# Left-over score tiles of two units in one step of four 64x64 products, and the ring loads issued in the table's order

## The chip, the cores and the metric

The kernel runs on one core of a Trainium2 chip. The metric is the device time of one execution in microseconds (us). Three runs of the kernel before gave 600.52 to 601.35 us, with a median of 600.97 us. The engines are PE (TensorE; PEld is its weight load), DVE (VectorE), ACT (ScalarE), POOL (GpSimd) and SP (SyncE), which issues every DMA here; SPq is SP's queue.

## The reference

Three layers stand one behind the other, all in float32. Attention has 4 batches of 8 heads, 576 rows and head size 64; its softmax keeps only scores within tau of the row's maximum. A soft mixture of 8 experts with 4 slots each follows, and then an MLP.

```python
scores = scale * np.matmul(q, k.transpose(0, 1, 3, 2))
thresh = np.max(scores, axis=-1, keepdims=True) - tau
scores = np.where(scores >= thresh, scores, -1e9)
attn = softmax(scores)                       # written out in the reference
x = (attn @ v), heads side by side           # 2304 x 512
d = softmax(x @ phi, axis=0); slots = d.T @ x
slot_out[e] = np.maximum(slots[e] @ w1[e], 0) @ w2[e]     # 8 experts
x = softmax(x @ phi, axis=1) @ slot_out
h = x @ w_in                                  # 2304 x 2048
return (h * sigmoid(1.702 * h)) @ w_out
```

## The kernel before

**Attention** (function `attention`) works in 16 units, each of two heads of a batch. A head has 576 query rows: four chunks of 128 and 64 left over. A unit therefore has nine score tiles of 128 x 576: tiles 0 to 7 are a chunk of one head, and tile 8 is the left-over 64 rows of both heads, one above the other. For each tile the stages are: scores on PE, row maximum with a copy to SBUF on DVE (`row_max`, RM), threshold on POOL (TH), exponential on ACT (`exps`, E), mask with row sum on DVE (`mask`, MK), transposes on PE (`trans`, T), their copies on ACT (C), then products with v on PE (`attn_v`, A; with the left-over rows of v, LV) and the division by the sums on DVE (VM).

`scores` (S0 to S3) computes two tiles at once: the two heads lie in partitions 0 to 63 and 64 to 127 of `qx` and `kx`, and their products of 64 contracted rows run as a pair, each head into a PSUM tile of its own (two banks a tile, two such tiles in all). The left-over tile (L) is made by one product of 128 contracted rows with `q_left`, a 128 x 128 matrix that holds the two heads' left-over queries on its diagonal and zeros elsewhere; `prep_rest` fills the diagonal by two ACT copies of 64 x 64. Each float32 product stands in the trace as two instructions.

**What sets the order.** The table `PLAN` gives every stage of a unit a place in tile times (columns: even unit, odd unit, last unit, first unit). The calls are sorted by it, and the instructions of PE, DVE, ACT and POOL are kept in that order by `tc.keep_in_program_order`. Loads that go through `load` are kept in that order on SP too. The loads of the expert weights into rings (`load_quarters`, line 101) are not: they stand where the scheduler puts them. The rings c, d, e, ... take SBUF that attention gives back (`swap`).

**After attention** come the experts (`experts`; `acc` on lines 1034 and 1076 is layer 1 and layer 2, with weights w_a to w_m streamed in) and the MLP (`ffn`, lines 1249 and 1275 to 1277). Decoding of w_in (`raw`, `top`, `y`, `wi`) is spread through attention.

Of the kernel before, what the change touches and what calls it, by code (L numbers as in the profile page):

```python
# [19 lines left out]
def kernel(  # L20
# [64 lines left out]
    def load_quarters(ring, n, spread=False):  # L85
# [3 lines left out]
        while i < n and quarters:  # L89
# [8 lines left out]
            if spread:  # L98
                slow.append(io)
            else:  # L100
                nc.sync.dma_start(**io)
# [42 lines left out]
    first = [True]  # L144

    def load(**io):
        ins = nc.sync.dma_start(**io)  # L147
        if first[0]:
            tc.keep_in_program_order(ins)
# [95 lines left out]
    def attention():  # L245
# [29 lines left out]
        q_left = [pl.tile([P, P], F32, name="q_left") for pl in stk]  # L275
        for t in q_left:
            ve.memset(t, 0.0)
# [49 lines left out]
        def turned(u, nm):  # L327


            if (u, nm) not in qk:  # L330
                n = C * P if nm == "q" else S + R
                qk[u, nm] = stk[u % 2].tile([P, n], F32, tag=nm, name=nm + "x")
            return qk[u, nm]

        def prep_rest(u, bank):
# [7 lines left out]
            def after():  # L343

                for h in range(2):
                    own = slice(h * R, (h + 1) * R)
                    ac.copy(out=q_left[u % 2][own, own], in_=t[own, 0, :])
# [5 lines left out]
        def prep_main(u, nm, bank):  # L353
# [7 lines left out]
            def after():  # L361
                src = t.rearrange("p c t -> p (c t)")
                if nm == "q":
                    ac.activation(
                        out=turned(u, nm), in_=src, func=AF.Copy, scale=neg if u else 1.0
# [36 lines left out]

        def weights(i):
            u, t = divmod(i, TPU)
            return p2[u, t // 2][:, t % 2 * S:(t % 2 + 1) * S]

        def scores(i):
# [13 lines left out]
            else:  # L421
                s_ps[i] = ps_s.tile([P, 2, 512], F32, tag="s", name="s_ps")
                prods = [(s_ps[i], q_left[u % 2], kx[:, R:])]
# [7 lines left out]
        def row_max(i):  # L431

            u, t = divmod(i, TPU)
            if (u, t // 2) not in p2:
                p2[u, t // 2] = pp[(u * (C + 1) + t // 2) % len(pp)].tile([P, 2 * S], F32, tag="p2", name="p2")
                mns[u, t // 2] = sm.tile([P, 2], F32, tag="mn", name="mn")
            mn2 = mns[u, t // 2]
            mn = mn2[:, t % 2:t % 2 + 1]
# [7 lines left out]
        def threshold(i):  # L446
            thr[i] = sm.tile([P, 1], F32, tag="th", name="th")
# [9 lines left out]
        def mask(i):  # L457
# [3 lines left out]
            if (u, half) not in l_sb:  # L461
                l_sb[u, half] = sm.tile([P, C + 1], F32, tag="l", name="l", bufs=2)
# [30 lines left out]
        def across(u, half):  # L493
# [8 lines left out]
            def after():  # L502
                row = l_row[u, half] = ptp.tile([P, 2 * P + R], F32, tag="l_row", name="l_row", bufs=2)
                ac.copy(out=row[:, 0:2 * P], in_=ps[:, 0:2 * P])
                for h in range(2 * half):
                    own = slice(h * D, (h + 1) * D)
                    ac.copy(out=row[own, 2 * P:], in_=ps[own, 2 * P + h * R:2 * P + (h + 1) * R])
# [11 lines left out]
        def trans(i):  # L519
# [6 lines left out]
            if i >= 140:  # L526
# [10 lines left out]
            if t == 2 * C:  # L537
# [7 lines left out]
                def after():  # L545
                    products_of(u, 1)
                    ac.copy(
                        out=pt[u, 1][:, :, :, 2 * P:].rearrange("p h c r -> p c h r"),
                        in_=ps.rearrange("p c (h r) -> p c h r", h=2),
                    )  # L550
# [841 lines left out]
```

## Time and profile before

| | us |
|---|---|
| median of 3 runs | 600.97 |
| the profiled execution | 601.18 |
| its span, first to last instruction | 599.0 |
| PE busy in the span | 582.7 (97%) |
| DVE busy | 400.5 (67%) |
| ACT busy | 374.1 (62%) |
| mean granted TensorE clock | 0.992 |

An engine's busy time is the sum of what its instructions cover. PE's matmuls are pipelined and overlap in the listing, so the time of a PE step is read from its start to the start of the next step, and not from its duration column. A releaser in brackets ("[1.06 <-ACT e_sb") is the idle time in front of an instruction and what ended it.

### The profile page before, as it was taken

Reading aid. Unit: us, or ns where it says so; the run is one execution under the profiler, and the core shown is the slowest. Engines: PE = TensorE matmul, PEld = TensorE weight load, DVE = VectorE, ACT = ScalarE, POOL = GpSimd, SP = SyncE. Lnnn points to the kernel's source line nnn. Section 1 sums busy time; section 2 is a strip of 40 time slices with the busy share of each in tenths; the row PEclk is TensorE's granted clock in tenths of the full one; section 3 lists DMA queues with packets and bytes.
Section 4 is the critical chain, followed back from the end, with each engine's and each line's share of the span. In section 5 each row is a group of like instructions: output and inputs, shape, how many; then the busy total and the mean of one; then the engine's idle time right before and its main releaser. Section 6 shows DMA issues by size and latency. Waiting matters only on the chain.

```text
span 599.0 us, 10535 instructions
## 1 busy us (share of the span) xinstructions
PE 582.7 (97%) x3712; PEld 414.1 (69%) x3712; DVE 400.5 (67%) x998; ACT 374.1 (62%) x804; POOL 140.9 (24%) x310
## 2 busy tenths in 40 slices
PE   7999999999999999999998998999999999999996
PEld 5666767667677676766765424778887788888884
DVE  3889899798997998878682435999981211512422
ACT  4788888788888798878861106767673354334330
POOL 1445445554455644222220100003000000000000
PEclk9899999999999999999999999999999999999999
DMA  7524054362542633420249993333310000200203
GB/s 223 136 74 124 21 161 144 88 180 92 161 143 62 172 125 80 138 75 24 87 150 369 410 409 144 134 120 130 138 37 0 1 0 1 105 1 0 106 0 106
DMA packets 63011, 69.94 MB, mean 117 GB/s; under 512 B 42736, under 2 KB 46832, under 8 KB 62960
## 3 DMA queue, kind: packets, MB, share of 16 engines
q1 hardware_dynamic: 62960, 69.28, 35.6%
q8 instruction: 29, 0.48, 0.3%
q14 instruction: 22, 0.18, 0.1%
HBM read 64.55 MB, written 4.72 MB: 116 GB/s over the span
## 4 chain that ended last, share of the span: by engine, by line
PE 87%; DVE 5%; DMA 3%; ACT 1%; SPq 1%; issue 1%; POOL 0%; DVEq 0%; POOLq 0%; ACTq 0%
PE s_ps L134 13%; PE o_ps L134 13%; PE y_ps L1275 11%; PE y_ps L1277 11%; PE y_ps L1276 11%; PE pt_ps L134 10%; PE r_ps L134 4%; PE h_ps L1249 3%; DVE p L134 3%; DMA w_c<-in_moe_w_dram 2%; PE acc L1034 2%; PE q_t L134 1%; SPq L147 1%; PE x_ps L134 1%; PE lg_ps L134 1%
## 5 line engine op out<-in xcount | busy, mean ns | idle before, releaser
L134 DVE SCALAR_TENSOR_TENSOR p<-p,th,e_sb 128x576 f32<-128x576 f32 x144 | 118.0, 841 | 13.5 <-ACT e_sb L134 11.4
L134 ACT ACTIVATE e_sb<-p,mn 128x576 f32<-128x576 f32 x144 | 110.7, 781 | 21.2 <-DVE p L134 20.3
L1275 PE MATMUL y_ps<-wo_h,gh 128*128 128x512 f32 x288 | 113.8, 396 | 0.0
L1276 PE MATMUL y_ps<-wo_l,gh 128*128 128x512 f32 x288 | 113.5, 394 | 0.0
L1277 PE MATMUL y_ps<-wo_h,gw 128*128 128x512 f32 x288 | 113.3, 395 | 0.0
L1238 DVE TENSOR_TENSOR gw<-sg,gh 128x768 fp32r<-128x768 f32 (+2 forms) x49 | 45.9, 939 | 91.9 <-ACT gh L1236 91.7
L134 DVE TENSOR_SCALAR_CACHE_REDUCE p<-s_ps 128x576 f32<-128x576 f32 x120 | 87.1, 751 | 10.3 <-PE pt_ps L134 6.6
L134 ACT COPY pt<-pt_ps 128x512 f32<-128x512 f32 x142 | 82.2, 586 | 17.8 <-PE pt_ps L134 17.1
L1254 ACT ACTIVATE sg<-h_ps 128x512 f32<-128x512 f32 (+1 forms) x96 | 42.5, 491 | 78.4 <-PE h_ps L1249 78.4
L134 PE MATMUL pt_ps<-ident,p 128*128 128x128 f32 x580 | 88.3, 280 | 0.5 <-DVE p L134 0.3
L134 PE MATMUL s_ps<-kx,qx 64*128 64x288 f32 x512 | 86.1, 438 | 2.2 <-DVE p L134 1.7
L134 PEld LDWEIGHTS pt_ps<-ident,p 128*128 128x128 f32 x580 | 65.3, 142 | 23.8 <-ACT ptr L134 5.4
L134 PE MATMUL o_ps<-pt,vn 128*64 128x320 f32 (+1 forms) x512 | 69.6, 412 | 0.3 <-ACT pt L134 0.3
L134 PEld LDWEIGHTS s_ps<-kx,qx 64*128 64x128 f32 x512 | 47.6, 189 | 25.0 <-issue 7.0
L1275 PEld LDWEIGHTS y_ps<-wo_h,gh 128*128 128x128 f32 x288 | 53.9, 187 | 14.1 <-ACT gh L1236 0.8
L1277 PEld LDWEIGHTS y_ps<-wo_h,gw 128*128 128x128 f32 x288 | 53.8, 187 | 13.5 <-DVE gw L1238 0.2
L1276 PEld LDWEIGHTS y_ps<-wo_l,gh 128*128 128x128 f32 x288 | 54.0, 187 | 11.2
L134 PEld LDWEIGHTS o_ps<-pt,vn 128*64 128x64 f32 x512 | 33.7, 136 | 31.0 <-issue 10.6
L134 POOL TENSOR_TENSOR th<-mn,few 128x1 f32<-128x1 f32 x144 | 38.7, 278 | 68.3 <-DVE p L134 63.4
L1236 ACT CAST gh<-sg 128x768 fp32r<-128x768 f32 (+2 forms) x49 | 40.2, 823 | 1.2
L134 POOL COPY lw<-l 128x256 f32<-128x256 f32 (+1 forms) x48 | 21.7, 472 | 34.8 <-PE r_ps L134 17.2
L134 ACT ACTIVATE y<-raw 128x256 f32<-128x256 f32 (+1 forms) x44 | 24.3, 551 | 8.9 <-DMA raw<-in_moe_w_out_dram 6.5
(189 smaller groups left out, 743.3 us busy)
## 6 DMA issues: line engine op xcount, KB each, us to landing
raw<-in_moe_w_out_dram SPq DMA_DIRECT2D x16, 512.0 KB, 3.3
raw<-in_moe_w_in_dram SPq DMA_DIRECT2D x24, 256.0 KB, 2.9
w_a<-in_moe_w_dram SPq DMA_DIRECT2D x12, 512.0 KB, 4.4
w_a<-in_moe_w_dram SPq DMA_DIRECT2D x6, 1024.0 KB, 13.8
qn<-in_q_dram SPq DMA_DIRECT2D x16, 256.0 KB, 3.7
kn<-in_k_dram SPq DMA_DIRECT2D x16, 256.0 KB, 4.0
vn<-in_v_dram SPq DMA_DIRECT2D x16, 256.0 KB, 2.9
w_m<-in_moe_w_dram SPq DMA_DIRECT2D x6, 512.0 KB, 5.0
```

The costliest lines, as they stand in the source:

```text
L134: ins = call(*args, **kw)
L147: ins = nc.sync.dma_start(**io)
L1034: nc.tensor.matmul(acc1[j][kc * NS:(kc + 1) * NS, :], s_in[kc // 2][:, kc % 2, e * NS:(e + 1) * NS], w_rows[1, e, kc][:, j * 512:(j + 1) * ...
L1236: nc.scalar.copy(out=gh[:, a], in_=sg[:, a])
L1238: nc.vector.tensor_sub(out=gw[:, a], in0=sg[:, a], in1=gh[:, a].bitcast(F32))
L1249: nc.tensor.matmul(ps, ws[:, f * P:(f + 1) * P], cs[:, t:t + n, :].rearrange("p t n -> p (t n)"), start=True, stop=True,)
L1254: nc.scalar.activation(out=part, in_=ps, func=AF.Gelu_apprx_sigmoid)
L1275: nc.tensor.matmul(ys[t], gh[:, tk], w_h, start=first, stop=False)
L1276: nc.tensor.matmul(ys[t], gh[:, tk], w_l, start=False, stop=False)
L1277: nc.tensor.matmul(ys[t], gw[:, tk], w_h, start=False, stop=last)
```

## The change

The left-over tiles of an even unit and of the odd unit behind it are computed in one step, at the even unit's L. Each head is now a 64 x 64 product: 64 contracted rows, 64 output rows. In the odd unit the heads go to exchanged halves of the PSUM tile, so that the four products have four different pairs of input half and output half. `q_left` and its zeros are gone; the left-over queries are 64 more columns of `qx`, filled by one ACT copy per unit. Behind the odd unit's left-over tile the copies of its transposes swap the heads back (two copies of 128 x 4 x 64 in place of one of 128 x 4 x 2 x 64), and the last unit's uses the ordinary PSUM tile. The two tiles share one p2 buffer, which is now taken in the order of use, and mn, th and l get more buffers. `load` chains every load to the one before it by a dependency without a semaphore, and the rings' loads go through it. All numbers of `PLAN` are new.

```diff
--- before.py
+++ after.py
@@ -98,7 +98,7 @@
             if spread:
                 slow.append(io)
             else:
-                nc.sync.dma_start(**io)
+                load(**io)
             for x in range(m):
                 for k in range(rows):
                     w_rows[layer, e, (j + x) * rows + k] = dst[:, x, k, :]
@@ -141,12 +141,18 @@
     te, ve, ac, po = (InOrder(x) for x in (nc.tensor, nc.vector, nc.scalar, nc.gpsimd))
-    first = [True]
+    first, newest = [True], [None]
     def load(**io):
-        ins = nc.sync.dma_start(**io)
+        ins = nc.sync.dma_start(**io).ins
         if first[0]:
-            tc.keep_in_program_order(ins)
+            if newest[0]:
+                tc.add_manual_dep(
+                    ins, newest[0], mybir.DependencyInfo(
+                        mybir.DependencyClass.NoSync, mybir.DependencyReason.DATA
+                    ), reason="loads in the order of the table",
+                )
+            newest[0] = ins.name
     w_in_v = w_in.bitcast(U32).rearrange("(k p) (f t) -> p k f t", p=P, t=2)
     w_out_v = w_out.bitcast(U32).rearrange("(k p) (d t) -> p k d t", p=P, t=2)
@@ -272,9 +278,6 @@
         v_left = ldv.tile([P, P], F32, name="v_left", bufs=1)
         ve.memset(v_left, 0.0)
-        q_left = [pl.tile([P, P], F32, name="q_left") for pl in stk]
-        for t in q_left:
-            ve.memset(t, 0.0)
         xt = tx.tile([P, HP, C * P], F32, name="xt")
         xtr = tx.tile([P, HP, 2 * R], F32, name="xtr")
         x_sb = tl.tile([P, C, DM], F32, name="x_sb")
@@ -328,7 +331,7 @@
             if (u, nm) not in qk:
-                n = C * P if nm == "q" else S + R
+                n = S if nm == "q" else S + R
                 qk[u, nm] = stk[u % 2].tile([P, n], F32, tag=nm, name=nm + "x")
             return qk[u, nm]
@@ -342,9 +345,7 @@
             def after():
-                for h in range(2):
-                    own = slice(h * R, (h + 1) * R)
-                    ac.copy(out=q_left[u % 2][own, own], in_=t[own, 0, :])
+                ac.copy(out=turned(u, "q")[:, C * P:], in_=t[:, 0, :])
                 ends = turned(u, "k").rearrange("p (e n) -> p e n", n=R)[:, 0::S // R, :]
                 ac.copy(out=ends, in_=t[:, 1:2, :].to_broadcast([P, 2, R]))
@@ -362,7 +363,7 @@
                 src = t.rearrange("p c t -> p (c t)")
                 if nm == "q":
                     ac.activation(
-                        out=turned(u, nm), in_=src, func=AF.Copy, scale=neg if u else 1.0
+                        out=turned(u, nm)[:, 0:C * P], in_=src, func=AF.Copy, scale=neg if u else 1.0
                     )
                 else:
                     ac.copy(out=turned(u, nm)[:, R:S], in_=src)
@@ -400,9 +401,15 @@
+        def pair_of(i):
+
+            u, t = divmod(i, TPU)
+            return ((u, t // 2), t % 2) if t < 2 * C else ((u // 2, "left"), u % 2)
+
         def weights(i):
             u, t = divmod(i, TPU)
-            return p2[u, t // 2][:, t % 2 * S:(t % 2 + 1) * S]
+            pair, x = pair_of(i)
+            return p2[pair][:, x * S:(x + 1) * S]
         def scores(i):
@@ -419,8 +426,15 @@
                     for h, rows in enumerate(heads)
                 ]
             else:
-                s_ps[i] = ps_s.tile([P, 2, 512], F32, tag="s", name="s_ps")
-                prods = [(s_ps[i], q_left[u % 2], kx[:, R:])]
+
+                prods = []
+                for v_ in (u, u + 1):
+                    ps = s_ps[v_ * TPU + t] = ps_s.tile([P, 2, 512], F32, tag="s", name="s_ps")
+                    for h, rows in enumerate(heads):
+                        to = heads[(h + v_) % 2]
+                        prods.append(
+                            (ps[to], turned(v_, "q")[rows, C * P:], turned(v_, "k")[rows, R:])
+                        )
             for half in range(2):
                 for ps, lh, rh in prods:
                     te.matmul(
@@ -431,11 +445,11 @@
         def row_max(i):
             u, t = divmod(i, TPU)
-            if (u, t // 2) not in p2:
-                p2[u, t // 2] = pp[(u * (C + 1) + t // 2) % len(pp)].tile([P, 2 * S], F32, tag="p2", name="p2")
-                mns[u, t // 2] = sm.tile([P, 2], F32, tag="mn", name="mn")
-            mn2 = mns[u, t // 2]
-            mn = mn2[:, t % 2:t % 2 + 1]
+            pair, x = pair_of(i)
+            if pair not in p2:
+                p2[pair] = pp[len(p2) % len(pp)].tile([P, 2 * S], F32, tag="p2", name="p2")
+                mns[pair] = sm.tile([P, 2], F32, tag="mn", name="mn", bufs=6)
+            mn = mns[pair][:, x:x + 1]
             ve.tensor_scalar(
                 out=weights(i).rearrange("p (a b) -> p a b", a=2), in0=s_ps.pop(i)[:, :, 0:HS],
                 scalar1=1.0 if u and t < 2 * C else neg, scalar2=None, op0=ALU.mult, op1=ALU.min,
@@ -444,7 +458,7 @@
             m_neg[i] = mn
         def threshold(i):
-            thr[i] = sm.tile([P, 1], F32, tag="th", name="th")
+            thr[i] = sm.tile([P, 1], F32, tag="th", name="th", bufs=6)
             po.tensor_tensor(out=thr[i], in0=m_neg[i], in1=tau_p, op=ALU.add)
         def exps(i):
@@ -459,7 +473,7 @@
             u, t = divmod(i, TPU)
             half = min(t // C, 1)
             if (u, half) not in l_sb:
-                l_sb[u, half] = sm.tile([P, C + 1], F32, tag="l", name="l", bufs=2)
+                l_sb[u, half] = sm.tile([P, C + 1], F32, tag="l", name="l", bufs=4)
             col = t - half * C
             ve.scalar_tensor_tensor(
                 out=weights(i), in0=weights(i), scalar=thr.pop(i), in1=e_sb.pop(i),
@@ -504,7 +518,8 @@
                 ac.copy(out=row[:, 0:2 * P], in_=ps[:, 0:2 * P])
                 for h in range(2 * half):
                     own = slice(h * D, (h + 1) * D)
-                    ac.copy(out=row[own, 2 * P:], in_=ps[own, 2 * P + h * R:2 * P + (h + 1) * R])
+                    c0 = 2 * P + (h + u) % 2 * R
+                    ac.copy(out=row[own, 2 * P:], in_=ps[own, c0:c0 + R])
             return after
@@ -523,7 +538,7 @@
             c, h = divmod(t, 2)
             if t < 2 * C:
                 src = src[:, h * R:h * R + C * P]
-            if i >= 140:
+            if 140 <= i < NU * TPU - 1:
                 both = ps_s.tile([P, 2, 512], F32, tag="s", name="pt_ps")
                 ps = both[:, 0, :].rearrange("p (c t) -> p c t", c=C)
@@ -544,13 +559,19 @@
                 def after():
                     products_of(u, 1)
-                    ac.copy(
-                        out=pt[u, 1][:, :, :, 2 * P:].rearrange("p h c r -> p c h r"),
-                        in_=ps.rearrange("p c (h r) -> p c h r", h=2),
-                    )
-
-                    for ps2, own in ((pr_, slice(0, R)), (pr2_, slice(R, P))):
-                        ac.copy(out=ptr[u, 1][own, 2 * P:], in_=ps2[own, own])
+                    cols = [slice((h + u) % 2 * R, ((h + u) % 2 + 1) * R) for h in range(2)]
+                    if u % 2:
+                        for h in range(2):
+                            ac.copy(out=pt[u, 1][:, h, :, 2 * P:], in_=ps[:, :, cols[h]])
+                    else:
+                        ac.copy(
+                            out=pt[u, 1][:, :, :, 2 * P:].rearrange("p h c r -> p c h r"),
+                            in_=ps.rearrange("p c (h r) -> p c h r", h=2),
+                        )
+
+                    for h, ps2 in enumerate((pr_, pr2_)):
+                        own = slice(h * R, (h + 1) * R)
+                        ac.copy(out=ptr[u, 1][own, 2 * P:], in_=ps2[own, cols[h]])
                 return after
             if h == 1:
@@ -799,69 +820,69 @@
             load_quarters("a", 4, spread=True)
         load_quarters("m", 4, spread=True)
         PLAN = {
-            "S0": (6.950, 5.787, 5.920, -90.399), "S1": (9.687, 7.534, 9.426, -85.175),
...
+            "S0": (13.504, 13.115, 19.632, -90.245), "S1": (14.214, 16.807, 27.277, -84.069),
...
         }
         left_behind, todo = {}, []
@@ -902,7 +923,8 @@
                 at(key("IV"), load_v, u)
             for j in range(C):
                 at(key(f"S{j}"), scores, u * TPU + 2 * j)
-            at(key("L"), scores, u * TPU + 2 * C)
+            if u % 2 == 0:
+                at(key("L"), scores, u * TPU + 2 * C)
             for t in range(TPU):
                 i = u * TPU + t
                 at(key(f"RM{t}"), row_max, i)
```

**Rows of the order, PE in the middle of attention, before.** Around one left-over step; `pt_ps` and `r_ps` are transposes of the tiles p_..., x4 counts instructions of the program.

```order
L134 MATMUL r_ps<-ident,p_2258 128x128
L134 MATMUL pt_ps<-ident,p_2258 128x128 x4
L134 MATMUL o_ps<-ptr,v_left 128x320
L134 MATMUL pt_ps<-ident,p_2314 128x128 x4
L134 MATMUL r_ps<-ident,p_2314 128x128
L134 MATMUL pt_ps<-ident,p_2314 128x128 x4
L134 MATMUL s_ps<-kx,q_left 128x288 x2
L134 MATMUL pt_ps<-ident,p_2365 128x128 x4
L134 MATMUL r_ps<-ident,p_2365 128x128
L134 MATMUL r_ps<-ident,lw 128x128 x3
L134 MATMUL pt_ps<-ident,p_2365 128x128 x4
L134 MATMUL s_ps<-kx,qx 128x288 x4
```

There is one such step per unit, between transposes, and an S step (`s_ps<-kx,qx`) four rows on.

**The same place after.**

```order
L134 MATMUL s_ps<-kx,qx 128x288 x4
L134 MATMUL pt_ps<-ident,p_2287 128x128 x4
L134 MATMUL r_ps<-ident,p_2287 128x128
L134 MATMUL pt_ps<-ident,p_2287 128x128 x4
L134 MATMUL o_ps<-ptr,v_left 128x320
L134 MATMUL pt_ps<-ident,p_2362 128x128 x4
L134 MATMUL s_ps<-kx,qx 64x288 x8
L134 MATMUL lg_ps<-xt,phi_sb 32x128 x12
L134 MATMUL lg_ps<-xtr,phi_sb 32x128 x12
L134 MATMUL lg_ps<-xt,phi_sb 32x128 x4
L134 MATMUL lg_ps<-xtr,phi_sb 32x128 x4
L134 MATMUL o_ps<-pt,vn 64x256 x4
```

There is one step of eight 64-row products for two units, and none at the next unit.

**SP at the program's start, before.** Names with n are loads of q, k and v; raw is a piece of w_in; w_c is a ring.

```order
L147 DMA qkr<-in_k_dram 64x6x64
L101 DMA w_c<-in_moe_w_dram 128x4x1024
L147 DMA qn<-in_q_dram 128x8x64
L147 DMA kn<-in_k_dram 128x8x64
L147 DMA vn<-in_v_dram 128x2x256
L147 DMA v_left<-in_v_dram 64x64 x2
L147 DMA vn<-in_v_dram 128x2x256
L147 DMA raw<-in_moe_w_in_dram 128x512 x2
```

The 2 MB of w_c stand ahead of unit 1's q and k and of the first pieces of w_in.

**SP at the start, after.**

```order
L147 DMA qkr<-in_k_dram 64x6x64
L147 DMA qn<-in_q_dram 128x8x64
L147 DMA kn<-in_k_dram 128x8x64
L147 DMA vn<-in_v_dram 128x2x256
L147 DMA v_left<-in_v_dram 64x64 x2
L147 DMA vn<-in_v_dram 128x2x256
L147 DMA raw<-in_moe_w_in_dram 128x512 x2
```

w_c is no longer here; the other loads stand as they stood.

**SP at the end of attention, before.** v_left are the left-over rows of v of a unit.

```order
L147 DMA w_b<-in_moe_w_dram 128x1024
L147 DMA v_left<-in_v_dram 64x64 x2
L147 DMA vn<-in_v_dram 128x2x256 x2
L147 DMA v_left<-in_v_dram 64x64 x2
L101 DMA w_d<-in_moe_w_dram 128x2x1024
L147 DMA v_left<-in_v_dram 64x64 x2
L101 DMA w_e<-in_moe_w_dram 128x2x1024
```

w_d and w_e stand between the v_left loads of the last units.

**SP at the end of attention, after.**

```order
L147 DMA vn<-in_v_dram 128x2x256
L147 DMA v_left<-in_v_dram 64x64 x2
L147 DMA w_c<-in_moe_w_dram 128x4x1024
L147 DMA w_d<-in_moe_w_dram 128x2x1024
L147 DMA vn<-in_v_dram 128x2x256
L147 DMA v_left<-in_v_dram 64x64 x4
L147 DMA w_e<-in_moe_w_dram 128x2x1024
```

w_c has come here, with w_d right behind it; the last vn and the v_left of the last two units now stand behind w_d.

## Rows read from the trace of the kernel before

**Rows 1.** The page: its first line, the span.

```profile
span 599.0 us, 10535 instructions
```

**Rows 2.** Six stretches; busy time of PE, PEld, DVE, ACT, POOL; clock, DMA share, GB/s.

```profile
0.00:20.00 20.00, 16.70 (x69) 11.74 (x70) 9.07 (x29) 7.37 (x13) 1.92 (x10) 0.83 0.82 227
20.00:60.00 40.00, 38.32 (x273) 26.07 (x272) 36.15 (x102) 34.68 (x78) 22.25 (x48) 1.00 0.36 94
60.00:300.00 240.00, 240.00 (x1856) 167.66 (x1856) 205.84 (x594) 201.41 (x466) 103.09 (x234) 1.00 0.37 109
300.00:316.40 16.40, 15.66 (x138) 10.53 (x138) 12.46 (x38) 10.01 (x22) 4.33 (x11) 1.00 0.50 182
316.40:362.00 45.60, 42.16 (x377) 18.15 (x366) 15.38 (x53) 5.64 (x15) 2.83 (x3) 1.00 1.00 397
362.00:599.00 237.00, 229.84 (x1020) 179.95 (x1020) 121.58 (x185) 115.03 (x211) 6.46 (x4) 0.99 0.18 60
```

**Rows 3.** The chain that ended last: start, us, what; one piece near 350 us.

```profile
347.28 14.67 DMA w_c<-in_moe_w_dram
```

**Rows 4.** SP's issues near the end of attention: start, us, engine, line, out<-in, count.

```profile
287.73 0.37 SPq L101 DMA_DIRECT2D w_d<-in_moe_w_dram  x1
...
306.33 0.37 SPq L101 DMA_DIRECT2D w_e<-in_moe_w_dram  x1
...
316.41 0.93 SPq L101 DMA_DIRECT2D w_i<-in_moe_w_dram  x2
```

**Rows 5.** PE's timeline, steps of units 8 and 7: start, us, operation.

```profile
172.02 1.14 PE L134 MATMUL s_ps<-kx,q_left 128*128 128x288 f32 x4
173.00 0.60 PE L134 MATMUL pt_ps<-ident,p 128*128 128x128 f32 x4
173.43 0.27 PE L134 MATMUL r_ps<-ident,p 128*128 128x128 f32 x1
...
177.90 1.24 PE L134 MATMUL s_ps<-kx,qx 64*128 64x288 f32 x8
179.07 0.86 PE L134 MATMUL lg_ps<-xt,phi_sb 128*32 128x128 f32 x24
...
180.96 1.95 PE L134 MATMUL o_ps<-pt,vn 128*64 128x256 f32 x16
182.84 0.66 PE L134 MATMUL xr_ps<-ident,xtr 128*128 128x128 f32 x4
```

**Rows 6.** SP's issues at the start.

```profile
6.29 0.61 SPq L101 DMA_DIRECT2D w_c<-in_moe_w_dram  x1
...
7.74 3.38 SPq L147 DMA_DIRECT2D kn<-in_k_dram  x1
...
14.65 1.14 SPq L147 DMA_DIRECT2D v_left<-in_v_dram  x2
...
16.47 0.94 SPq L147 DMA_DIRECT2D raw<-in_moe_w_in_dram  x2
```

**Rows 7.** ACT's timeline at the start, with the idle time in brackets.

```profile
20.05 0.44 ACT L134 ACTIVATE y<-raw 128x256 f32<-128x256 f32 x1 [1.93 <-DMA raw<-in_moe_w_in_dram]
...
21.01 1.42 ACT L134 ACTIVATE e_sb<-p,mn 128x576 f32<-128x576 f32 x2
```

**Rows 8.** DVE's timeline at the start.

```profile
19.75 0.82 DVE L134 TENSOR_SCALAR_CACHE_REDUCE p<-s_ps,few 128x576 f32<-128x576 f32 x1 [1.29 <-PE s_ps L134]
...
21.87 0.82 DVE L134 SCALAR_TENSOR_TENSOR p<-p,th,e_sb 128x576 f32<-128x576 f32 x1 [1.06 <-ACT e_sb L134]
```

**Rows 9.** DMA issues: out<-in, count, KB each, median us to landing.

```profile
w_d<-in_moe_w_dram SPq DMA_DIRECT2D x1, 1024.0 KB, 4.9
...
v_left<-in_v_dram SPq DMA_DIRECT2D x32, 16.0 KB, 3.1
```

**Rows 10.** Groups by line and form, ACT's small copies: busy us, mean ns, idle.

```profile
L134 ACT COPY l_row<-r_ps 128x256 f32<-128x256 f32 x32 | 12.1, 379 | 2.3 <-PE r_ps L134 1.8
...
L134 ACT COPY q_left<-r_ps 64x64 f32<-64x64 f32 x32 | 6.6, 206 | 0.3
```

More of the change, by code (lines that the diff above doesn't have):

```diff
@@ L801, in attention @@
         PLAN = {
[59 rows of a table removed]
-            "XRS": (26.669, 26.669, 3086.227, 26.669), "CXRS": (26.995, 26.995, 3242.044, 26.995),
[3 rows of a table removed]
[59 rows of a table added]
+            "XRS": (34.783, 34.783, 3024.308, 34.783), "CXRS": (35.456, 35.456, 3176.694, 35.456),
[3 rows of a table added]
         }
```

122 rows, old and new, of the table PLAN are left out of this document.

## The prediction

> **What bounds the kernel now.** First the six stretches [rows 2]. From 60 to 300 us PE is busy in every microsecond, DVE in 205.84 of 240 (86%), ACT in 201.41 (84%): PE bounds the middle of attention, and each of the others has some 35 us left there. From 316.4 to 362 us the DMA share is 1.00 at 397 GB/s: this stretch is bound by the experts' weights. The chain of waits shows the same, a wait of 14.67 us for the last of them [rows 3]. That stream is held back by attention: w_i, the first large part of it, goes out at 316.41 us, when the last unit's products have given back their buffers [rows 4], and from there the DMA engines don't rest. So the stream ends earlier by as much as attention does, and the MLP behind it (237 us, [rows 2]) isn't touched. The first 60 us are another case: PE is busy 16.70 of 20 and 38.32 of 40 us, at a granted clock of 0.83 in the first stretch, so what holds there are waits between engines.
>
> The sum is made against the profiled execution, 601.18 us, of which the span is 599.0 [rows 1]. The median of the runs is 600.97, 0.2 lower, and the forecast is brought to it at the end.
>
> **The left-over step.** Before, each unit has one: from 172.02 to 173.00 us, 0.98 us [rows 5], so 1.96 for two units. It is twice 288 columns deep. After, two units share a step of eight products, sixteen instructions. If all four 64x64 products run beside each other, it is again twice 288 columns deep. The trace has no such step, so it is bounded by its neighbours. From below by the depth alone, 0.98. The S step, with two row halves beside each other and the same depth, takes 1.17 (177.90 to 179.07). If two of the four run beside each other and the other two come behind, it takes 2 x 1.17 = 2.34. That column tiles run beside each other is seen in o_ps: 16 instructions, eight products of 256 columns on two column halves, 1.88 us (180.96 to 182.84), which is close to the depth of four (4 x 256 columns at 0.98 us for 576 are 1.74). The count of instructions doesn't bound it: 64 of lg_ps take 1.89 us (179.07 to 180.96), 30 ns each [rows 5]. I take 1.2, by the S step: rows and columns each run side by side in this trace, and the four products have four different pairs of halves. That saves 0.76 us for two units. Fourteen of the sixteen left-over steps start behind 60 us, where PE bounds: 7 x 0.76 = 5.3 us. For the first pair, among waits, I count nothing.
>
> In the o_ps step the weights of both column halves go into the same rows, and its sixteen loads leave hardly a trace in the 1.88 us. The Trainium skill's page TensorE: Matmul & The Clock Gate (Part 3, The mechanism) says that a weight load overlaps a running matmul only when its row group differs; by that the two products of a row half would follow each other and the new step would take about 2.34, so the row speaks against the rule here, and the sum stays with the row.
>
> **The start.** SP issues w_c, 2 MB, at 6.29 us, and behind it the issue of kn takes 3.38 us, v_left goes out at 14.65 and the first pieces of w_in only at 16.47 [rows 6]. ACT waits 1.93 us for the first of them at 20.05, in front of the exponentials that start at 21.01 [rows 7], and DVE's mask at 21.87 waits 1.06 us for one of these [rows 8]. After, w_c is not there; with the issue times of the same rows (0.61 a load, 1.14 for v_left) the pieces go out near 10.3 and land, as before 3.6 us later, near 14, before ACT comes to them. The 1.06 us go. DVE also stands idle 1.29 us in front of 19.75 us, and in the new order two decode steps and a reciprocal fall into that idle time; I estimate that they fill half of it, 0.64. I count 1.7. From below it is nothing: the scores for which DVE waits at 19.75 come from PE at a lowered clock, and four copies for unit 1 now stand in front of an exponential on ACT, which may be late in its turn. From above: of the first 20 us, at a clock of 0.83, a third ran at 1.2 GHz (0.5 x 0.34 = 0.17); if none did, half of that third comes back, 3.4 us, and 4.5 with the 1.06.
>
> **w_c and w_d at the end of attention.** The new order has no wait for SBUF at w_c (it could be loaded at 6.29 us, so nothing lay there). It follows the v_left of unit 13 and is followed by w_d. In the trace of before w_d goes out at 287.73, and the next large load, w_e, at 306.33 [rows 4]: 18.6 us with 1 MB to move. Two more MB, 5.3 us at 397 GB/s, fit there, at no cost; they'd cost up to 5.3 if they were issued behind w_e's time. The dependencies that keep the order hold no semaphore, so they add no wait by themselves. But w_d waits for the even unit's last scores, and behind it on SP now stand vn of the last unit and v_left of the last two. w_d takes 4.9 us to land, a v_left 3.1 [rows 9]; queued one behind the other, the v_left of unit 14 is there about 6 us behind the left-over step. PE's next reader of it stands behind two half o_ps steps (2 x 0.94) and 30 transposes of 0.11 each (four from 173.00 to 173.43), 5.2 us. So a new wait of about 0.8; part of it is made good in the tail, and I count +0.5, between 0 and 2.
>
> **Small parts.** ACT loses 32 copies of 206 ns, 6.6 us [rows 10], and gets 16 of twice the partitions and, for eight odd units, one copy more behind the transposes; by the copies of 128x256 (379 ns) these are at most 16 x 0.38 + 8 x 0.38 = 9.1 us and by those of 206 ns 4.9. ACT has 39 us free in the middle, which hides either. The two memsets on DVE stand before the load of tau that it waits for. More buffers for mn, th and l take waits away, none on PE's path.
>
> **The new table.** Every stage has a new place, and what that costs can't be read from the trace of before. In the new order PE has at least one o_ps step (1.88 us) or as many transposes between two score steps, and DVE needs two row maxima (0.82 each, [rows 8]) to free the PSUM tiles for the next: that fits. I take 0, with 2 us less and 5 more as ends.
>
> The sum: -5.3 - 1.7 + 0.5 = -6.5, so 594.7 for an execution like the profiled one, and **594.5** against the median.
>
> **Rivals.**
> - DVE or ACT takes PE's place. With PE 2% shorter, in-order waits on them could eat what PE gains. For it: DVE is at 86% and 90% in 20 to 60 us. Against it: 34 us of idle in the middle, and its work doesn't grow. Term 1 goes: -1.7 + 0.5, about 599.8.
> - The four products don't all overlap because two row halves write one PSUM bank. Before, each head of an S step has a PSUM tile of its own; in the new step both heads of a unit share one, on different partitions. If they exclude each other, the products of a half run as h0, then h1 with the other unit's h0, then the last, which can join the next half's first: five passes of 0.49 us (half of 0.98) and the 0.2 that the S step shows above its depth, 2.65 us against 1.96. Seven pairs lose 0.69 each, 4.8; with -1.7 and +0.5 it ends at 604.6, slower. It decides from a step of over 2.1 us. Against it: in lg_ps four column tiles write one bank side by side. The Trainium skill states the rule in TensorEngine Tiling (Array Packing), Restrictions and Gotchas: row tiles can't access one bank at the same time; no row here shows two row tiles in one bank.
> - Two products run, the other two follow: 2.34 us, 7 x 0.38 = 2.7 lost, 602.5.
> - The clock at the start stays at 2.4 GHz and the new order has fewer waits: 4.5 instead of 1.7 and the 2 of the table: about 590.
> - w_c isn't hidden: +5.3, about 599.8.
>
> **Chances.** The forecast 0.58 (its own range 592.5 to 596.5), DVE or ACT 0.13, one bank 0.08, two and two 0.05, the better start 0.12, w_c 0.04. From 590 to 600.5 the range leaves out the two slow cases and the edge of the best. A measurement here can tell about 0.2% (1.2 us) from no change: faster by more is the forecast, the best case and half of the first rival, 0.77; the other half and w_c make 0.09; slower 0.14.
>
> **What the profile after should show.** Eight left-over steps of sixteen instructions, each about 1.2 us from its start to the next step's; over 2 us would prove a rival. The w_in pieces issued near 10 us, and no wait of ACT for them. w_c issued before 300 us. w_i issued near 310 us, the same wait of some 14 to 15 us for the last weights, and the same 237 us for the MLP. The forecast is wrong if PE is no longer busy throughout the middle, or if w_i goes out later than 314 us.

## The result, and the profile after

The changed kernel takes 593.45 us (median; 593.34 to 594.56) against 600.97 (600.52 to 601.35): a ratio of 0.9879 with a 95% interval of 0.9862 to 0.9897. Two later series, each with runs of the kernel before beside it, gave 0.9885 (0.9867 to 0.9903) and 0.9865 (0.9843 to 0.9887). The gain is 7.5 us where 6.5 were forecast. The profiled execution takes 593.42 us.

The page of the changed kernel, its span and PE's line (busy us, share of the span, instructions), beside [rows 1]:

```profile
span 591.6 us, 10597 instructions
PE 575.0 (97%) x3776; PEld 405.2 (68%) x3776; DVE 401.3 (68%) x996; ACT 372.8 (63%) x796; POOL 157.6 (27%) x310
```

PE is busy 575.0 us instead of 582.7, and the span is 7.4 shorter. Its six stretches, cut at the corresponding events (w_i goes out at 308.92), with the columns of [rows 2]:

```profile
0.00:20.00 20.00, 17.36 (x106) 12.26 (x108) 12.54 (x38) 12.16 (x25) 6.02 (x19) 1.00 0.58 141
20.00:60.00 40.00, 40.00 (x307) 27.31 (x304) 37.81 (x108) 34.46 (x77) 24.23 (x45) 1.00 0.38 104
60.00:293.00 233.00, 230.98 (x1862) 157.54 (x1861) 202.21 (x580) 195.73 (x448) 111.75 (x228) 1.00 0.42 119
293.00:308.90 15.90, 14.46 (x125) 9.75 (x129) 11.84 (x35) 9.99 (x23) 6.27 (x12) 1.00 0.48 171
308.90:355.00 46.10, 42.57 (x378) 18.29 (x369) 15.31 (x53) 5.45 (x15) 2.83 (x3) 1.00 1.01 400
355.00:591.60 236.60, 229.68 (x1020) 180.06 (x1016) 121.60 (x185) 115.03 (x211) 6.48 (x4) 0.99 0.18 60
```

The last two are as before (45.6 and 237.0 us). All of the gain stands in front of w_i, which goes out at 308.92 instead of 316.41. Three differences are seen against [rows 2]. In the first 20 us the clock is 1.00, not 0.83, and DVE does 12.54 us of work in place of 9.07. From 20 to 60 us PE no longer waits at all. From 60 to 293 us it now does wait, 2.0 us in sum, where it had not before. The chain of waits still runs through the experts' weights [rows 3], as it did:

```profile
322.63 16.84 DMA w_a<-in_moe_w_dram
339.48 15.32 DMA w_c<-in_moe_w_dram
```

PE's timeline at a left-over step, beside [rows 5] (start, us, operation, count):

```profile
163.19 1.20 PE L134 MATMUL s_ps<-kx,qx 64*64 64x288 f32 x16
164.32 0.86 PE L134 MATMUL lg_ps<-xt,phi_sb 128*32 128x128 f32 x24
```

The step of two units takes 1.13 us from its start to the next, against 2 x 0.98. SP's queue at the start [rows 6] no longer holds w_c, and ACT's decoding of w_in [rows 7] follows without a wait:

```profile
7.08 0.65 SPq L147 DMA_DIRECT2D kn<-in_k_dram  x1
...
8.70 1.14 SPq L147 DMA_DIRECT2D v_left<-in_v_dram  x2
...
10.51 0.94 SPq L147 DMA_DIRECT2D raw<-in_moe_w_in_dram  x2
```

```profile
15.32 0.77 ACT L134 ACTIVATE y<-raw 128x256 f32<-128x256 f32 x2
```

The issue of kn takes 0.65 us instead of 3.38. At the end of attention SP issues as follows [rows 4]. The line of v_left sums up four issues, from the first one's start to the last one's end: the pair of unit 14 goes out at 279.14 us, the pair of unit 15 at 290.20.

```profile
258.04 0.58 SPq L147 DMA_DIRECT2D w_c<-in_moe_w_dram  x1
278.00 0.37 SPq L147 DMA_DIRECT2D w_d<-in_moe_w_dram  x1
278.73 0.37 SPq L147 DMA_DIRECT2D vn<-in_v_dram  x1
279.14 12.16 SPq L147 DMA_DIRECT2D v_left<-in_v_dram  x4
...
308.92 0.93 SPq L147 DMA_DIRECT2D w_i<-in_moe_w_dram  x2
```

And PE's timeline there:

```profile
276.72 1.20 PE L134 MATMUL s_ps<-kx,qx 64*64 64x288 f32 x16
...
285.29 0.67 PE L134 MATMUL o_ps<-ptr,v_left 128*128 128x256 f32 x2 [1.58 <-DMA v_left<-in_v_dram]
285.89 1.24 PE L134 MATMUL s_ps<-kx,qx 64*128 64x288 f32 x8
```

PE stands still for 1.58 us until the v_left of unit 14 is there; the chain of waits gives 5.48 us for that transfer (279.67 to 285.15). So the change gives something back at this place. In the kernel before, the left-over step of unit 14 starts here:

```profile
286.53 1.14 PE L134 MATMUL s_ps<-kx,q_left 128*128 128x288 f32 x4
```

It now starts 9.8 us earlier (276.72), but w_i only 7.5. From this step to w_i it was 29.9 us and is 32.2.

### The profile page after: what moved, and what is told of

It reads as the page before. It is cut to its first block, busy times and chain, and to the rows that moved or that the text cites. A ratio compares the mean times of both kernels' runs of the same rounds, so it can differ in the third digit from the quotient of the medians.

```text
span 591.6 us, 10597 instructions
## 1 busy us (share of the span) xinstructions
PE 575.0 (97%) x3776; PEld 405.2 (68%) x3776; DVE 401.3 (68%) x996; ACT 372.8 (63%) x796; POOL 157.6 (27%) x310
## 4 chain that ended last, share of the span: by engine, by line
PE 84%; DMA 7%; DVE 4%; ACT 1%; issue 1%; POOL 1%; SPq 0%; POOLq 0%; DVEq 0%
PE s_ps L134 13%; PE o_ps L134 13%; PE y_ps L1297 11%; PE y_ps L1299 11%; PE y_ps L1298 11%; PE pt_ps L134 10%; PE r_ps L134 4%; PE h_ps L1271 3%; DVE p L134 3%; DMA w_a<-in_moe_w_dram 3%; DMA w_c<-in_moe_w_dram 3%; PE x_ps L134 1%; PE k_t L134 1%; PE q_t L134 1%; PE lg_ps L134 1%
## 5 line engine op out<-in xcount | busy, mean ns | idle before, releaser
L134 DVE SCALAR_TENSOR_TENSOR p<-p,th,e_sb 128x576 f32<-128x576 f32 x144 | 123.5, 871 | 4.8 <-ACT e_sb L134 3.4
L134 PE MATMUL s_ps<-kx,qx 64*128 64x288 f32 (+1 forms) x640 | 92.4, 427 | 1.2 <-DVE p L134 0.6
L134 POOL TENSOR_TENSOR th<-mn,few 128x1 f32<-128x1 f32 x144 | 63.3, 449 | 110.0 <-DVE p L134 104.1
L134 ACT COPY pt<-pt_ps 128x512 f32<-128x512 f32 (+1 forms) x150 | 82.6, 567 | 14.7 <-PE pt_ps L134 13.4
L134 PE MATMUL pt_ps<-ident,p 128*128 128x128 f32 x578 | 85.7, 278 | 1.0 <-ACT pt L134 0.6
L134 PE MATMUL o_ps<-pt,vn 128*64 128x320 f32 (+1 forms) x512 | 70.9, 414 | 0.3
L134 PEld LDWEIGHTS s_ps<-kx,qx 64*128 64x128 f32 (+1 forms) x640 | 50.6, 175 | 23.9 <-issue 8.3
L134 POOL COPY lw<-l 128x256 f32<-128x256 f32 (+1 forms) x48 | 26.1, 563 | 5.2 <-DVE l L134 4.0
```

The costliest lines, as they stand in the source:

```text
L134: ins = call(*args, **kw)
```

## The experiments

Each series had its own runs of the kernel before beside it, with medians of 601.14, 602.28 and 602.62 us. So runs of different series are compared by their ratio to these. The first series (w_c ahead of the loads, the order of the loads alone, the transposes moved, w_d moved for the first time) holds no run of the changed kernel. For each execution the mean granted clock is known as well; it is a mean over the whole execution, and only a profiled execution shows where in it the clock fell.

**The four quadrants.** The odd unit's heads are not exchanged, so that the two units use the same two quadrants:

```diff
-                        to = heads[(h + v_) % 2]
+                        to = heads[h]
```

(and `(h + u) % 2` becomes `h` in the copies behind it.)

> The changed kernel with the heads of the odd unit not exchanged: the four products of the left-over step have two pairs of halves, each used by both units. Theory (the gain of the step is that four different quadrants run beside each other, and PE bounds the middle): the products of the second unit come behind those of the first, the step takes 2.0 to 2.4 us instead of 1.13, and eight times 0.9 to 1.2 us come on top: 600.5 to 603. Rival (another engine bounds the middle by now, since DVE is busy over 90% from 20 to 300 us): the step takes as long, but less than 4 us come on top, under 597.5. Second rival (the quadrants don't matter): the step stays at 1.13, 593.4.

```profile
208.09 2.16 PE L134 MATMUL s_ps<-kx,qx 64*64 64x288 f32 x16
210.17 1.08 PE L134 MATMUL o_ps<-pt,vn 128*64 128x256 f32 x8
```

The step takes 2.08 us, 0.95 more. The time is 601.22 us (ratio 0.9979, 0.9963 to 0.9995) beside 595.26 for the changed kernel in the same series: 6.0 us of the 7.0 gained there go with the exchange. From the first left-over step to that of unit 14 stand 264.7 us (18.8 to 283.5) against 258.2 in the changed kernel's trace of that series (18.9 to 277.1). Seven steps of 0.95 are 6.65, and 6.5 arrive. PE bounds the middle; the first rival of the prediction falls. (DVE, which the expectation puts at over 90%, is busy 202.21 of 233 us there, 87%.) The eighth step, unit 14's own, costs nothing: from there to w_i it is 32.2 us in both, since the wait for v_left (0.60 us here, 1.58 there) covers it. Behind w_i single executions differ, of one kernel too: the first profiled execution of the changed kernel ends 284.5 us after w_i goes out, the second 286.0. So the profiled execution of this run, the fastest of its twelve, ends only 3.9 us behind that of the changed kernel in its series, although its w_i goes out 6.4 later.

**The same products twice.** Each half of the left-over step is issued a second time.

```diff
-            for half in range(2):
+            for half in [0, 1] * (1 + t // (2 * C)):
```

> The changed kernel with each left-over step's sixteen instructions issued twice in a row, with the same result. It adds 8 x 1.1 us to PE and to no other engine. Theory (PE bounds the middle of attention and nothing else is late): 7 to 9 us longer, 600.5 to 602.5. Rival (waits on DVE and ACT take over when PE is shorter, so that a good part of what the left-over step saved was never on the path): 3 to 6 us longer, 596.5 to 599.5.

```profile
169.34 2.17 PE L134 MATMUL s_ps<-kx,qx 64*64 64x288 f32 x32
171.44 0.86 PE L134 MATMUL lg_ps<-xt,phi_sb 128*32 128x128 f32 x24
```

The step takes 2.10 us, and the time is 601.90 (ratio 1.0002, 0.9986 to 1.0017), 6.6 more than the changed kernel: the time lies in the theory's range, the difference between its 7 to 9 and the rival's 3 to 6. From the first left-over step to that of unit 14 it is 264.9 us, 6.3 more than in the profiled execution of the changed kernel that has the same fall of the clock (258.6, below), where seven steps of 0.97 are 6.8. So lengthening the step arrives nearly in full without any change of the heads, too.

**The order of issue in the step.** The even unit's eight instructions first, then the odd one's:

```diff
-            for half in range(2):
-                for ps, lh, rh in prods:
+            for half, group in [(half, g) for g in (prods[:2], prods[2:]) for half in range(2)]:
+                for ps, lh, rh in group:
```

> The changed kernel with the sixteen instructions of the left-over step in another order: both halves of the even unit first, then both halves of the odd one (before, the four products of a half follow each other). Theory (a product runs beside another only if it is issued while that one runs, and the queue is in order): two of four quadrants are in use at a time, the step takes 1.96 to 2.35 us, 8 x 0.83 to 1.2 more: 600 to 603. Rival (the products of the odd unit catch up, since their quadrants are free from the start): 1.13 to 1.4 us, 593.4 to 595.5.

```profile
163.52 1.21 PE L134 MATMUL s_ps<-kx,qx 64*64 64x288 f32 x16
164.66 0.54 PE L134 MATMUL lg_ps<-xt,phi_sb 128*32 128x128 f32 x12
```

1.14 us and 594.36 (ratio 0.9873, 0.9848 to 0.9897): no difference. My theory of a queue that has to bring the four together was wrong. In these runs a busy quadrant doesn't hold up products for another one (1.14 us), and only the sharing of quadrants costs (2.08).

**w_c ahead of the loads again, in the changed kernel.**

```diff
-                load(**io)
+                nc.sync.dma_start(**io)
```

(and `load` is that of the kernel before.)

> The changed kernel, but the rings' loads stand outside the chain again, so w_c (2 MB) goes out near 6.3 us, ahead of the loads of unit 1 and of w_in. Theory (the order of the loads is worth something at the start): the first pieces of w_in go out near 16.5 us again instead of 10.5 and land near 20, ACT waits for them some 4 to 5 us where it now comes to them at 15.3; 2 to 5 us longer than the changed kernel, 595.5 to 598.5. Rival (the new order of PE at the start does it alone, the loads have no part): within 0.5 us of the changed kernel, 593 to 594, with the clock at 1.00 in the first 20 us. Second rival (w_c at 258 us harms the tail): shorter than the changed kernel by up to 2.

ACT's timeline, PE's, and the stretch from 20 to 60 us:

```profile
20.14 0.43 ACT L134 ACTIVATE y<-raw 128x256 f32<-128x256 f32 x1 [4.18 <-DMA raw<-in_moe_w_in_dram]
```

```profile
21.81 1.11 PE L134 MATMUL k_t<-ident,kn 128*128 128x128 f32 x4 [4.26 <-ACT pt L134]
```

```profile
20.00:60.00 40.00, 38.19 (x275) 26.18 (x276) 35.94 (x100) 34.07 (x78) 23.71 (x45) 0.92 0.32 81
```

599.49 us (ratio 0.9973, 0.9957 to 0.9988): 1.7 us of the gain are left, fewer than any of the three expectations had. ACT waits 4.18 us for w_in, PE stands still for 4.26 in turn, and while it does the clock falls, to 1.2 GHz from 19.9 to 26.7 us. The new table brings little with the old order of the loads. The second rival, on the tail, falls as to the total. A small part of it isn't excluded: from unit 14's left-over step to w_i it is 31.5 us here, against 32.2 in the first profile of the changed kernel and 31.6 in its third.

**The order of the loads alone, in the kernel before.** The line above is exchanged the other way, with the new `load`; table, steps and copies stay.

> The kernel before, with nothing but the rings' loads put into the chain; the order of PE, DVE, ACT and POOL is that of before. Theory (the granted clock falls because PE stands still in front of its score steps at 9.0 and 11.4 us, which the loads don't touch): the clock falls as before, 0.83 in the first 20 us, and only DVE's wait of 1.06 us for ACT and part of what follows goes: 0.5 to 1.5 shorter than before, 599.5 to 600.5. Rival (the loads of w_c, or what they delay, make the clock fall): clock 1.00 in the first 20 us and 3 to 4.5 us shorter, 596.5 to 598.

```profile
0.00:20.00 20.00, 16.80 (x64) 12.22 (x66) 8.83 (x28) 7.94 (x15) 3.82 (x13) 0.76 0.52 123
```

The median is 599.45 us (ratio 0.9968, 0.9950 to 0.9986), but twelve executions spread over 5 us and go by their clock: five of 0.990 take 600.3 to 601.5, four of 0.993 598.8 to 599.5, three of 0.994 and 0.995 596.5 to 597.2. The profiled one, 601.22 us, has the fall and no gain at all. The kernel before in the same series doesn't go by its clock: 20 executions of 0.987 to 0.990 take 600.3 to 603.1, and four of 0.992 to 0.996 take 600.6 to 602.6. So each theory held for a part of the executions. The fall comes without w_c ahead of the loads as well (the profiled execution), so w_c isn't what makes it. That it costs time only once the loads are early is read from the mean clocks and the times, not from a trace of a fast execution.

**PE's idle time in the kernel before.** Four transposes stand between S1 and S2 of the first unit:

```diff
-            "T0": (13.644, 11.593, 74.667, -65.051)
+            "T0": (13.644, 11.593, 74.667, -77.5)
```

> The kernel before, with one step moved in the first unit: the four transposes of tile 0 stand on PE between the score steps S1 and S2 instead of behind S2, as in the changed kernel. Theory (PE's idle time of 0.92 us in front of S2 is what the clock falls after): the transposes fill that idle time, the clock stays at 1.00 in the first 20 us, S2 and S3 take 2.0 instead of 3.0 and 2.3; 2 to 3.5 us shorter than before, 597.5 to 599. Rival (the clock falls for another reason): 600.5 to 601.5, clock 0.83 as before. Second rival (the clock stays, but the loads of w_in then hold ACT at 20 us and eat it): clock 1.00 and 600 to 601.

```profile
19.84 0.43 ACT L134 ACTIVATE y<-raw 128x256 f32<-128x256 f32 x1 [3.68 <-DMA raw<-in_moe_w_in_dram]
```

```profile
22.93 0.48 PE L134 MATMUL r_ps<-ident,qkr 128*128 128x128 f32 x1 [3.52 <-ACT ptr L134]
```

```profile
0.00:20.00 20.00, 16.42 (x79) 11.16 (x79) 9.57 (x30) 7.51 (x14) 2.03 (x11) 1.00 0.80 228
20.00:60.00 40.00, 36.77 (x242) 24.77 (x242) 32.94 (x93) 32.28 (x73) 21.03 (x46) 0.91 0.32 81
```

601.73 us (ratio 1.0016, 1.0002 to 1.0030). The clock stays at 1.00 up to 20 us, and nothing is won: ACT comes to w_in earlier and waits 3.68 us for it instead of 1.93 [rows 7], PE then stands still for 3.52 (up to 22.93), and the clock falls near the end of that, from 22.4 to 29.3 us. It is the second rival of this run, with a later fall on top. With the experiment before, this points to two limits at the start, each of which hides the other; both removed in the kernel before was not run.

**w_d behind the v_left of unit 14, in the changed kernel.**

```diff
+        floor[0] = max(floor[0], TPU * (NU - 2) + PLAN["VL"][0]) + 0.0001
         at(floor[0], swap, even_units, "d", 2)
```

> The changed kernel, but w_d goes out behind the v_left of unit 14 instead of ahead of it (nothing else moves). Theory (v_left of unit 14, 5.5 us in flight behind w_d's 1 MB, makes PE wait 1.58 us at 285 us, and the products that were pulled ahead of it cost the rest of a give-back of some 3 us): the wait goes, 1.5 to 3 us shorter than the changed kernel, 590.5 to 592. Rival (the tail is held by DVE, ACT and POOL behind it, which swallow the 1.58): within 0.5 us of it, 593 to 594.

```profile
279.47 1.20 PE L134 MATMUL s_ps<-kx,qx 64*64 64x288 f32 x16
...
286.30 0.60 PE L134 MATMUL o_ps<-ptr,v_left 128*128 128x256 f32 x2
286.82 1.24 PE L134 MATMUL s_ps<-kx,qx 64*128 64x288 f32 x8
```

The wait is gone, and w_i goes out 30.4 us behind the left-over step (309.86) instead of 32.2. (This profiled execution has the fall of the clock at the start, the one with 32.2 hasn't; with the fall the changed kernel has 31.6.) The median is 592.78 us (ratio 0.9865, 0.9849 to 0.9881). That alone is too near to the changed kernel, so both ran again in one series:

> The changed kernel once more, as the measure for the two that follow: 593.3 to 595.3, with some executions whose mean clock is under 0.994 and most above.

> The kernel with w_d behind the v_left of unit 14 once more, directly beside the changed kernel. In the profile its w_i goes out 30.4 us behind the last left-over step, against 32.2. Theory (the 1.8 us are on the path to the end, since the experts' stream starts at w_i): 1.3 to 1.8 us under the changed kernel at the same mean clock. Rival (DMA traffic in the experts' stretch takes it back): within 0.5 us.

594.33 us (0.9865, 0.9843 to 0.9887) and 592.60 (0.9836, 0.9811 to 0.9860): 1.7 less, though the intervals still overlap. The two profiled executions both have the fall at the start: w_i goes out at 311.39 and 309.84, and they take 596.19 and 594.41. Other executions of the same mean clock don't all agree: at 0.997 it is 594.1 to 594.4 against 592.60, but at 0.995 it is 592.49 against 593.18, the other way. So the medians and the traces speak for this version, by 1.2 us from the left-over step to w_i; the runs don't settle the size.

**The fall at the start in the changed kernel.**

> The changed kernel itself, beside the three that follow, for the spread of its granted clock. The same start (no instruction differs in the first 250 us) had a clock of 1.00 throughout in one execution, 593.4 us, and 0.83 in the first 20 us in the profiled execution of the kernel with w_d behind v_left, 594.4. Theory (the time goes by whether the clock falls at the start, and that is decided by chance): executions of mean clock 0.996 or more at 593.3 to 593.8, those of 0.990 at 595 to 596.5. Rival (a fall at the start is hidden, as in the kernel before, whose executions of 0.989 and of 0.993 take the same 601): 593.3 to 594.5 at any clock.

595.26 us. Its executions don't follow the theory: 0.989 took 595.67, but 1.000 took 595.28. The profiled one (1.000) issues w_i at 309.25, 0.3 later than the first profile, and loses the other 1.5 us behind that. A clearer case came with the series in which w_d was moved a second time. Its profiled execution of the changed kernel has the fall, from 10.1 to 17.0 us:

```profile
0.00:20.00 20.00, 17.35 (x78) 12.88 (x79) 9.77 (x30) 9.33 (x19) 4.18 (x16) 0.83 0.51 123
```

```profile
279.78 1.20 PE L134 MATMUL s_ps<-kx,qx 64*64 64x288 f32 x16
...
287.76 0.67 PE L134 MATMUL o_ps<-ptr,v_left 128*128 128x256 f32 x2 [0.99 <-DMA v_left<-in_v_dram]
```

The left-over step of unit 14 comes 3.1 us later than without the fall, w_i (311.39) 2.5 later, since the wait for v_left is then 0.99 instead of 1.58; the execution takes 596.19, 2.8 more than the first profiled one.

**PE filled in front of S0 and S1** (in the version with w_d moved):

```diff
         first_unit()
+        warm(4)
...
+            if u == 0:
+                at(key("S0") + 0.001, warm, 5)
```

> The kernel with w_d behind v_left, and nine matmuls of 128x128 on the identity in PE's two idle times of 0.57 and 0.64 us in front of S0 and S1 of the first unit. Theory (a fall of the clock near 11 us follows these idle times): no execution falls there, the mean clock is 0.996 or more in all of them and the time is 591.5 to 593.5. Rival (the fall comes in some executions whatever PE does in these two idle times, or follows the first 1.35 us, in which PE has nothing): the same spread of clocks as without them, 0.989 to 1.000, and the same times; if the matmuls come late they delay S1 by up to 0.5 us.

```profile
7.68 1.16 PE L134 MATMUL r_ps<-ident 128*128 128x128 f32 x8 [0.85 <-ACT kx L134]
```

593.62 us (ratio 0.9859, 0.9836 to 0.9882), with clocks of 0.993 to 0.998; both the time and the lowest clock miss the theory's ranges. The profiled execution has no fall at the start (its only one before the last few us is from 317.0 to 320.4 us), but S1 starts at 11.25 us instead of 9.68: the first added matmuls wait 0.85 us for ACT, and S0 and S1 wait for the added ones. It is 1.0 us slower than the version without them (592.60). Whether the fall was prevented or only didn't come stays open with five executions.

## Why the prediction was right, and where it wasn't

**The left-over step** was right: 1.13 us against 1.2, 0.83 a pair against 0.76, and the path follows it (6.5 of 6.65 us with the heads kept). I counted seven pairs because the first lies among waits at the start; the one that doesn't count is the last. Seven of 0.83 are 5.8 (forecast 5.3). The two rivals on overlap fall: both heads of a unit write one PSUM bank, from two row halves, and the step takes 1.13 us, not 2.65; and two products of one row half overlap too, or it would be 2.34. The Trainium skill's rule that row tiles can't use one bank at the same time (TensorEngine Tiling (Array Packing), Restrictions and Gotchas) isn't borne out by the 1.13 us, where they write different partitions of it.

**The start** was the step that failed most. I counted 1.7: DVE's 1.06 and half of 1.29 us. At unit 14's left-over step the changed kernel leads by 9.8 us, of which 5.8 are the left-over steps, so that start and new table together made 4.0 in the profiled execution; with the fall of the clock it is 6.7 and 0.9. Start and table can be told apart at unit 2's left-over step, before and after:

```profile
60.21 1.14 PE L134 MATMUL s_ps<-kx,q_left 128*128 128x288 f32 x4
```

```profile
53.70 1.20 PE L134 MATMUL s_ps<-kx,qx 64*64 64x288 f32 x16
```

The lead is 6.5 us there already; less one pair's 0.83, the start made 5.7. In the execution with the fall this step starts at 56.61, and the start made 2.8. My ends were 0 and 4.5: the start without a fall lies beyond them. I took the clock's fall for a cost that was there and would in part stay. In the kernel before, a clock of 1.00 up to 20 us won nothing, because ACT couldn't pass the 20 us at which w_in landed (the run with the transposes moved, which then had a later fall). In the changed kernel w_in is early, and between its profiled executions with and without the fall w_i differs by 2.5 us; the times of the other executions don't sort by their mean clock as clearly.

**w_c and w_d.** That w_c is hidden was right as far as the trace shows (it goes out at 258.04, and nothing waits for this load; the w_c in the chain at 339.48 is a later one). The new wait behind w_d came where it was named, with the wrong size: I counted 0.5, between 0 and 2, and the way to w_i grew by 2.3. Landing times before [rows 9], and now, between 276 and 300 us:

```profile
w_d<-in_moe_w_dram SPq DMA_DIRECT2D x1, 1024.0 KB, 5.5
...
vn<-in_v_dram SPq DMA_DIRECT2D x1, 256.0 KB, 5.3
v_left<-in_v_dram SPq DMA_DIRECT2D x4, 16.0 KB, 3.7
```

I had put the v_left of unit 14 at 6 us behind the left-over step's end; the chain lets it land at 285.15, 7.3 behind it (277.85). It had 5.48 us in flight instead of the 3.1 I used. A transfer of 16 KB behind 1 MB of w_d and 256 KB of vn takes as long as these. The Trainium skill's page DMA: Bandwidth & Descriptors (Queues, rings and completion order) says that each DMA engine takes the descriptors of a queue in their order; the 5.48 us agree with that. The wait is 1.58 us. Moving w_d gives back 1.2 us of the way to w_i where both executions have the fall (31.6 and 30.4). The prediction's sign that PE is no longer busy throughout the middle came up here: it stands still for 2.0 of the 233 us, and 1.58 of them are this wait.

**The new table** at nothing was wrong by 1.7. From unit 2's left-over step to unit 14's the lead grows by only 3.3 us (6.5 to 9.8), where six pairs at 0.83 would give 5.0. From start to start, PE's left-over steps take 11.7 us before and 6.8 after in this stretch, but the same other steps take 214.6 before and 216.2 after. They take 216.4 in the execution with the fall and 216.3 in the run with the heads kept, so this belongs to the new order and not to one execution. Of it, 0.4 us is idle time of PE; what makes the rest stays open.

**Small parts** at nothing were right as far as the trace shows: ACT's sum is 372.8 us (374.1 before).

The sum, seen from w_i: -5.8 for the left-over steps, -5.7 for the start, +1.7 for the new table, +2.3 for the tail, -7.5. The forecast had -5.3, -1.7, 0 and +0.5. That the total came out within 1.1 us is luck as far as these three go: the start brought 4.0 more than I counted, table and tail took back 3.5. (In the chances, half of the first rival and w_c make 0.105, not 0.09, and the slower cases 0.13, not 0.14.)

## What to carry to other kernels

Where an engine waits for a transfer, a slower engine in front of it can cost little, and removing one of the two may show little: here the old order of the loads took nearly 6 us from the new table, but in the old table the new order gave 1.7 in the median, and four transposes moved to keep PE busy gave none. Products of 64 contracted and 64 output rows ran best here on both halves, rows and columns, each running product on a quadrant of its own: four took 1.13 us, and 2.08 where two shared a quadrant. A new order of the instructions is not free even where PE hardly waits: here it took back 1.6 us of the 4.9 that the shorter steps saved in the middle. A small load that somebody waits for goes ahead of the large prefetch, not behind it (here 5.48 us in flight behind it).

## What the runs showed of the hardware

The same instructions have the fall of TensorE's clock in one execution and not in the next (the changed kernel: none in two profiled executions, one from 10.1 to 17.0 us in the third). What went ahead of it differs. The four transposes of k before S0, in the first profile and in the one with the fall:

```profile
5.43 0.66 PE L134 MATMUL k_t<-ident,kn 128*128 128x128 f32 x4
5.92 0.27 PE L134 MATMUL r_ps<-ident,qkr 128*128 128x128 f32 x1
```

```profile
5.79 1.06 PE L134 MATMUL k_t<-ident,kn 128*128 128x128 f32 x4
6.64 0.32 PE L134 MATMUL r_ps<-ident,qkr 128*128 128x128 f32 x1
```

From start to start they take 0.49 us in the one and 0.85 in the other. At a clock of 1.00 four such transposes take 0.43 [rows 5]; so in the one the clock had risen to 2.4 GHz by then, and in the other it was still at 1.2. In the traces of the new order that have the loads early and no added matmuls, all four with 0.82 to 0.85 have a fall near 10 us, and the four with 0.44 to 0.50 have none. That goes together in eight executions; that the one brings the other is not shown. The Trainium skill's page TensorE: Matmul & The Clock Gate (Part 1, What's actually happening) says that the gate's window runs on regardless of when a kernel starts, so that the moment of a change differs from run to run; this agrees with the two executions above. A single profile of this kernel can therefore be 2 to 3 us off the next one (593.42 and 596.19 us).
